# Mask rows as twelve codes, a maximum pass that writes, and last outputs in single banks

## The chip, the cores and the metric

The kernel runs on one core of a Trainium2 chip. Its time is the device time of one execution in microseconds. Three runs of the kernel before took 771.14, 771.51 and 772.78 us, so the median is 771.51. The engines are TensorE (PE, with its weight loads shown apart as PEld), VectorE (DVE), ScalarE (ACT), GpSimd (POOL) and SyncE (SP), which only issues DMAs.

## The reference

Attention over 2 batches and 8 heads of 768 tokens with 64 features, in which a query sees only keys of its own hash bucket, and then two MLPs over the 1536 tokens:

```python
q_bits = (np.einsum('bhsd,dk->bhsk', q, proj) > 0)        # 6 bits; k_bits likewise
mask = q_bucket[:, :, :, None] == k_bucket[:, :, None, :] # bucket = the 6 bits as a number
scores = np.where(mask, scale * q @ k.T, -1e9)
attn = np.exp(scores - max(scores)); attn /= attn.sum() + 1e-9
x = attn @ v
h = x @ w_in;  x = (h - tanh(h)) @ w_out                  # 512 -> 2048 -> 512
h = x @ w_in2; x = (h * sigmoid(1.702 * h)) @ w_out2
```

## The kernel before, in words

Every large product is made from numbers split in two parts, a high one in TensorE's fast 32-bit format (`xh`, `wh`, `ka`, `qa`) and the rest (`xl`, `wl`), with the product of the two rests left out.

**Attention.** The 16 heads run as eight pairs. A pair has twelve steps, one for each head and each 128 queries; 96 steps in all. In iteration `s` of the loop TensorE does in this order: the score products of step `s + 2` (`scores`, L334: four of 384 columns, the first two from `qa`/`ka`, the last two from `qb`/`kb`), two of the twelve products of probabilities and values of an earlier half pair (`pv`, L388; each shows as two matmuls), and six 128x128 transposes of the probabilities of step `s` (`transposes`, L369). VectorE takes the maximum of a step's 768 scores from PSUM (L348) and makes a bias of it (`nb`, L350). ScalarE takes the exponential from PSUM, with that bias, into `pr` in SBUF, with the sum over the row (L352), and copies the transposes from PSUM to SBUF (L377). The scores lie in one of two PSUM tiles of two banks each (tag `S`), the transposes in two single banks (tag `T`); tags `g` and `v` have a bank each. Tiles of one tag take turns, and a tile is given out again when all that reads it is done.

**The mask** is part of the score product. `qa` and `ka` hold 128 rows: the 64 features twice over in different parts. `qb` and `kb` hold 64 feature rows and, in rows 64 to 127, one row for each of the 64 buckets: a one in `kb` where the key lies in that bucket, and minus 2 to the 100 in `qb` where the query does not. A key of another bucket so gets a score of about minus 2 to the 100. The rows are made once a pair. `prep_bits` multiplies keys and queries by `proj` into a PSUM tile `pb` (L262) and compares with zero on VectorE (`bits`, L271). `prep_hot`, four times a pair, multiplies the bits with a table (`sel_sb`, loaded at the start) into a PSUM tile `po` (L293), and VectorE makes 384 columns of `kb` and of `qb` from it (L305, L308). The first pair is made another way, from a small table in bf16, and the change leaves that alone.

**Preparation of the next pair** (`prep_ahead`): at step 10 of a pair the tiles of the pair after next are loaded (`r` on SP, `ka`, `qa`, `qb` on GpSimd's queue); at step 1 GpSimd splits the rest parts off (`split_q`, `split_k`, four operations of 64x768, L238 and L244) and `prep_bits` is done; `prep_hot` follows in steps 2, 4, 5 and 7; `v` is loaded in step 7. For the second pair it is step 3 and then 4 to 7. Slices of the MLP weights are loaded and converted in between. `r` has one buffer, the others two.

**The MLPs** run over 16 slices `c` of the hidden units, eight for each layer, with 3 blocks `t` of 512 tokens and 2 halves `j` of a slice. The order of all work is a list written out by hand (`ORDER`, and `STEADY` where it has no entry): `h21` is the product into the hidden block t = 2, j = 1; `t21` its activation, `g21` the gate, `hi21` and `lo21` its two parts; `o213` the output product for t = 2, j = 1 and feature block d = 3 (or token block, in the last layer), three matmuls of 512 columns (L703); `ev23` adds the output to the sum `acc` on VectorE (L711) and, in the last slice, stores it (L714). A name with `-` belongs to the slice before. An output block's four accumulators lie in two `S` tiles, two in each. Where the list has `P`, products are combined from sums of blocks, which the change does not touch.

```python
ORDER[16] = "ev10- ev11- ev12- ev13- g21- hi21- o200- o201- o202- o203- lo21- o210- o211- "
            "o212- o213- ev20- ev21- ev22- ev23- "          # what follows the last slice
```

Of the kernel before, what the change touches and what calls it, by code (L numbers as in the profile page):

```python
# [10 lines left out]
F32 = mybir.dt.float32  # L11
F32R = mybir.dt.float32r
# [24 lines left out]
CH = 2  # L37
NCHUNK = 2 * NFC // CH
BIG = float(2.0**100)
NTAB = 98  # L40
# [17 lines left out]
def lsh_attention_then_two_mlps(  # L58
# [4 lines left out]
    rr: bass.AP,  # L63
    vv: bass.AP,
    tab: bass.AP,
    sel: bass.AP,
    eye: bass.AP,
    w1: bass.AP,
    w2: bass.AP,
# [118 lines left out]
    sel0 = tab_sb[:, 32:96].bitcast(BF16)  # L188
    pop_sb = tab_sb[:, 96:97]
    hot_sb = tab_sb[:, 97:98]  # L190
    eye_sb = cst.tile([128, 128], F32, name="eye_sb")
    sel_sb = cst.tile([128, 4, 128], F32R, name="sel_sb")

# [18 lines left out]
    def load_first():  # L212
        b, p = pairs[0]
        pair_tiles(0)
        qa, qb, ka, kb, r = heads[0]
        c0, c1 = slice(0, HALF), slice(HALF, S)
        for h in range(2):
            nc.sync.dma_start(out=r[:, h], in_=rr[b, p, :, h])
            nc.gpsimd.dma_start(out=ka[:, h], in_=kd[b, p, :, h])
            nc.gpsimd.dma_start(out=qa[:, h, c0], in_=qd[b, p, :, h, c0])  # L220
            nc.gpsimd.dma_start(out=qb[0:64, h, c0], in_=qd[b, p, 0:64, h, c0])
        nc.sync.dma_start(out=eye_sb, in_=eye)
        nc.gpsimd.dma_start(out=qa[:, :, c1], in_=qd[b, p, :, :, c1])
        nc.gpsimd.dma_start(out=qb[0:64, :, c1], in_=qd[b, p, 0:64, :, c1])
        nc.gpsimd.dma_start(out=sel_sb, in_=sel)

    def load_v(i):
        b, p = pairs[i]
# [23 lines left out]
    def prep_bits(i, hs=(0, 1), tag="g"):  # L252
        r = heads[i][4]
        pb = ps.tile([128, 512], F32, tag=tag, name=f"pb{i}_{hs[0]}")
        if hs[0] == 0:
            bits[i] = sm.tile(
                [128, HALF], F32R if i else BF16, tag=f"bits{min(i, 1)}", name=f"bits{i}", bufs=1
            )
# [11 lines left out]
        rows = slice(hs[0] * 64, hs[-1] * 64 + 64)  # L270
        nc.vector.tensor_scalar(bits[i][rows], pb[rows, :HALF], 0.0, None, op0=ALU.is_gt)  # L271

    def prep_hot(i, h, f, tag="g"):
        qa, qb, ka, kb, r = heads[i]
        c = slice(f * HALF, (f + 1) * HALF)  # L280
        g = 64 * h + 32 * f
        po = ps.tile([128, 512], F32, tag=tag, name=f"po{i}_{h}_{f}")
        if i == 0:
            nc.tensor.matmul(
                po[:, :HALF],
                sel0[g : g + 32],
                bits[i][g : g + 32],
                start=True,
                stop=True,
                tile_position=(g, 0),  # L290
            )
        else:
            nc.tensor.matmul(po[:, :HALF], sel_sb[:, g // 32], bits[i], start=True, stop=True)  # L293

        def masks():
            if i == 0:
                nc.scalar.activation(
                    kb[64:128, h, c], po[64:128, :HALF], AF.Relu, bias=hot_sb[64:128], scale=BIG
                )
                nc.vector.tensor_scalar(  # L300
                    qb[64:128, h, c], po[0:64, :HALF], pop_sb[0:64], -1.0,
                    op0=ALU.subtract, op1=ALU.max,
                )
                return
# [22 lines left out]
    def scores(s):  # L327
        u, i, f, j, h = where(s)
        qa, qb, ka, kb, _ = heads[i]
        t0 = f * UT + j * QT  # L330
        sc = ps.tile([128, 2, 512], F32, tag="S", name=f"sc{s}", bufs=2)
        for n in range(2):
            for hf in range(2):
                nc.tensor.matmul(  # L334
                    sc[:, hf, :HALF],
                    (qa, qb)[n][:, h, t0 : t0 + QT],
                    (ka, kb)[n][:, h, hf * HALF : (hf + 1) * HALF],
                    start=(n == 0),
                    stop=(n == 1),
                )  # L340
        return sc

    def softmax(s, sc):
        u, i, f, j, h = where(s)
        if s % (2 * NQ) == 0:
            sums[u] = sm.tile([128, NQ, 2], F32, tag="rs", name=f"rs{u}")
        nm = sm.tile([128, 1], F32, tag="nm", name=f"nm{s}")
        nc.vector.tensor_reduce(nm, sc[:, :, :HALF], AX.XY, ALU.max, negate=True)  # L348
        nb = sm.tile([128, 1], F32, tag="nb", name=f"nb{s}")
        nc.vector.tensor_scalar_mul(nb, nm, D**-0.5)  # L350
        pr = prp.tile([128, S], F32, tag="pr", name=f"pr{s}")
        nc.scalar.activation(  # L352
            pr.rearrange("p (a b) -> p a b", a=2), sc[:, :, :HALF], AF.Exp,
            bias=nb, scale=D**-0.5, accum_out=sums[u][:, j, h : h + 1],
        )
        prob[s] = pr

# [100 lines left out]
    PO = ((2, 4, 5, 7), (4, 5, 6, 7))  # L458
# [5 lines left out]
    masks = [prep_hot(0, 0, 0, "g"), prep_hot(0, 0, 1, "v")]  # L464
    masks[0]()
    split_q(0, 0, nc.vector, c0)
    masks[1]()
# [6 lines left out]
    for s in range(NSTEP + 2 * NQ + 1):  # L474
# [22 lines left out]
        if s < NSTEP:  # L497
            if s == 0:
                for f in range(2):
                    prep_hot(0, 1, f, "gv"[f])()  # L500
# [12 lines left out]
            convert(s, 1)  # L513
# [167 lines left out]

    def out_mm(c, t, j, d):
        first = j == (1 if t == 1 and c % LAYER else 0)
        if first and d == 0:
            oacc[c, t] = [
                ps.tile([128, 2, 512], F32, tag="S", name=f"o{c}_{t}_{i}", bufs=2)
                for i in range(2)
            ]
        hi, lo = gh[c, t, j], gl[c, t, j]
        woh, wol = wh[c, j], wl[c, j]  # L690
        o = oacc[c, t][d // 2][:, d % 2, :]
# [12 lines left out]

    def evac(c, t, d):
        o = oacc[c, t][d // 2][:, d % 2, :]
        m = acc_of(d, t)
        if c % LAYER == 0:
            nc.scalar.activation(m, o, AF.Copy)  # L709
# [48 lines left out]
    def issue(name, c):  # L758
# [39 lines left out]
        elif kind == "tab":  # L798
# [60 lines left out]
        ),  # L859
        NCHUNK: (  # L860
            "ev10- ev11- ev12- ev13- g21- hi21- o200- o201- o202- o203- lo21- o210- o211- "
            "o212- o213- ev20- ev21- ev22- ev23- "
        ),
    }
    for c in range(NCHUNK + 1):
        for name in ORDER.get(c, STEADY).split():
# [69 lines left out]
```

## Time and profile before

| | |
|---|---|
| runs (3), median | 771.51 us (771.14 to 772.78) |
| profiled execution, own time | 772.15 us |
| its span | 770.0 us |
| PE busy / DVE / ACT / POOL | 749.5 / 585.1 / 424.3 / 400.6 us |
| first score product / first MLP product | 9.45 / 257.17 us |
| last matmul starts | 764.33 us |
| reduction L348, exponential L352, mask L305 + L308 | 91.6, 87.0, 17.5 + 17.1 us |

A row of the timeline has the start, the duration, the engine, the line, the operation, the tile written and the tiles read, their shape, and in brackets how long the engine had been idle before and what ended that. Matmuls overlap, and their ends are modelled; what a matmul costs is read from the distance of starts. A row that says x2 merges two instructions that follow each other.

### The profile page before, as it was taken

The page shows a single profiled execution, that of the slowest core. Times are in us where ns is not written, and L with a number is a line of the kernel's source. Part 1 is how long each engine was busy: PE and PEld are TensorE (multiplying, and loading weights), DVE is VectorE, ACT ScalarE, POOL GpSimd, SP SyncE. Part 2 cuts the span into 40 slices and gives each one's busy share as a digit, 9 for nine tenths or more (in the row PEclk, how much of TensorE's full clock was granted, in tenths as well). Part 3 has the DMA queues.
Part 4 walks back from the last instruction along what each step waited for, and adds up shares of the span by engine and source line. Part 5 has one row for each costly group of instructions (what it writes and reads, how often), then busy time and mean ns, then how long its engine had stood idle before and what let it go on. Part 6 is the DMA issues. An engine that isn't in the chain of part 4 may idle for free.

```text
span 770.0 us, 10036 instructions
## 1 busy us (share of the span) xinstructions
PE 749.5 (97%) x3708; PEld 570.0 (74%) x3708; DVE 585.1 (76%) x840; ACT 424.3 (55%) x793; POOL 400.6 (52%) x342
## 2 busy tenths in 40 slices
PE   5899999999999999999999999999999999999996
PEld 3566666666666688888888888887888888888885
DVE  4778778767667768878887787897798778877653
ACT  3777777777778466354353543656545355353430
POOL 6451651643410586564644745699774474564620
PEclk9999999999999999999999999999999999999999
DMA  9535234043120211131112111302022211130004
GB/s 266 177 104 192 88 104 163 22 145 125 40 76 1 110 55 66 45 110 54 55 66 83 72 55 54 110 6 104 24 87 78 81 60 55 55 110 0 1 11 154
DMA packets 12993, 62.89 MB, mean 82 GB/s; under 512 B 1616, under 2 KB 2512, under 8 KB 8848
## 3 DMA queue, kind: packets, MB, share of 16 engines
q1 hardware_dynamic: 8928, 46.21, 16.7%
q0 software_dynamic: 3872, 15.99, 7.1%
q8 instruction: 29, 0.48, 0.3%
q14 instruction: 20, 0.16, 0.1%
q10 hardware_dynamic: 144, 0.05, 0.0%
HBM read 59.10 MB, written 3.15 MB: 81 GB/s over the span
## 4 chain that ended last, share of the span: by engine, by line
PE 88%; DVE 3%; POOL 2%; issue 2%; DMA 2%; ACT 1%; POOLq 0%; DVEq 0%; ACTq 0%
PE o L703 31%; PE h L614 12%; PE y L614 10%; PE pv L388 10%; PE tp L369 9%; PE sc L334 8%; PE w L614 5%; PE x L614 2%; DMA r<-in_rr 1%; DMA ka<-in_kd 1%; POOL xl L726 1%; PE rb L413 1%; PE pb L262 1%; PE po L293 1%; DVE acc L594 1%
## 5 line engine op out<-in xcount | busy, mean ns | idle before, releaser
L676 POOL TENSOR_TENSOR gl<-f,gh 128x512 fp32r<-128x512 f32 x62 | 86.2, 1390 | 162.1 <-ACT gh L671 156.7
L711 DVE TENSOR_TENSOR acc<-o,acc 128x512 f32<-128x512 f32 x168 | 108.6, 684 | 48.6 <-PE o L703 48.1
L377 ACT ACTIVATE pt<-tp 128x384 f32<-128x384 f32 x184 | 80.3, 489 | 47.9 <-PE tp L369 47.0
L348 DVE TENSOR_REDUCE nm<-sc 128x1 f32<-128x768 f32 x96 | 91.6, 954 | 14.6 <-PE sc L334 13.4
L369 PEld LDWEIGHTS tp<-eye_sb,pr 128*128 128x128 f32 x576 | 61.6, 140 | 53.5 <-issue 25.7
L145 POOL TENSOR_TENSOR wl<-w,wh 128x512 fp32r<-128x512 f32 (+1 forms) x62 | 86.4, 1405 | 19.0 <-ACT wh L142 18.9
L352 ACT ACTIVATE pr<-sc,nb 128x768 f32<-128x768 f32 x96 | 87.0, 906 | 16.0 <-DVE nb L350 8.9
L369 PE MATMUL tp<-eye_sb,pr 128*128 128x128 f32 x576 | 83.5, 281 | 0.0
L388 PE MATMUL pv<-pt,v 128*64 128x384 f32 x384 | 82.0, 510 | 0.0
L735 ACT ACTIVATE u<-y 128x512 f32<-128x512 f32 x42 | 25.2, 600 | 100.6 <-PE y L614 100.6
L703 PE MATMUL o<-wh,gh 128*128 128x512 f32 x192 | 75.0, 391 | 0.9 <-ACT acc L709 0.7
L703 PE MATMUL o<-wh,gl 128*128 128x512 f32 x192 | 74.8, 390 | 0.5 <-POOL gl L676 0.5
L703 PE MATMUL o<-gh,wh 128*128 128x512 f32 x192 | 74.8, 390 | 0.0
L703 PE MATMUL o<-wl,gh 128*128 128x512 f32 x192 | 74.7, 389 | 0.0
L703 PE MATMUL o<-gl,wh 128*128 128x512 f32 x192 | 74.7, 389 | 0.0
L703 PE MATMUL o<-gh,wl 128*128 128x512 f32 x192 | 74.7, 389 | 0.0
L614 PE MATMUL h<-xl,wh 128*128 128x512 f32 x160 | 62.4, 390 | 0.6 <-POOL xl L726 0.6
L614 PE MATMUL h<-xh,wh 128*128 128x512 f32 x160 | 62.4, 390 | 0.0
L614 PE MATMUL h<-xh,wl 128*128 128x512 f32 x160 | 62.3, 389 | 0.0
L334 PE MATMUL sc<-ka,qa 128*128 128x384 f32 x192 | 55.7, 371 | 2.3 <-DVE qa L238 1.9
L671 ACT ACTIVATE gh<-f 128x512 fp32r<-128x512 f32 x62 | 39.0, 629 | 28.7 <-DVE f L667 28.5
L334 PE MATMUL sc<-kb,qb 128*128 128x384 f32 x192 | 50.2, 342 | 2.0 <-DVE qb L300 2.0
(138 smaller groups left out, 1652.7 us busy)
## 6 DMA issues: line engine op xcount, KB each, us to landing
raw<-in_w SPq DMA_DIRECT2D x32, 1024.0 KB, 4.8
ka<-in_kd POOLq DMA_DIRECT2D x7, 768.0 KB, 4.7
qa<-in_qd POOLq DMA_DIRECT2D x7, 768.0 KB, 6.7
r<-in_rr SPq DMA_DIRECT2D x7, 768.0 KB, 4.5
v<-in_vv SPq DMA_DIRECT2D x8, 384.0 KB, 3.1
out<-acc SPq DMA_DIRECT2D x12, 256.0 KB, 2.1
qb<-in_qd POOLq DMA_DIRECT2D x7, 384.0 KB, 8.0
r<-in_rr SPq DMA_DIRECT2D x2, 384.0 KB, 4.2
```

The source lines that it names most:

```text
L145: nc.gpsimd.tensor_tensor(wl[c, j][:, f], ws[c, j][:, f], wh[c, j][:, f].bitcast(F32), ALU.subtract)
L334: nc.tensor.matmul(sc[:, hf, :HALF], (qa, qb)[n][:, h, t0 : t0 + QT], (ka, kb)[n][:, h, hf * HALF : (hf + 1) * HALF], start=(n == 0), stop ...
L348: nc.vector.tensor_reduce(nm, sc[:, :, :HALF], AX.XY, ALU.max, negate=True)
L352: nc.scalar.activation(pr.rearrange("p (a b) -> p a b", a=2), sc[:, :, :HALF], AF.Exp, bias=nb, scale=D**-0.5, accum_out=sums[u][:, j, h : ...
L369: nc.tensor.transpose(tp[:, k * 128 : (k + 1) * 128], pr[:, c * 128 : (c + 1) * 128], eye_sb)
L377: nc.scalar.activation(dst, src, AF.Copy)
L388: nc.tensor.matmul(acc[u][h * 64 : (h + 1) * 64, :UT], v[:, h, c, :], probT[u][:, c, h, :], start=(c == 0), stop=(c == NCH - 1),)
L614: nc.tensor.matmul(o, a, b, start=(start and n == 0 and m == 0), stop=(n == len(pairs) - 1 and m == 2), skip_group_check=not start,)
L671: nc.scalar.activation(gh[c, t, j], fs[c, t, j], AF.Copy)
L676: eng.tensor_tensor(gl[c, t, j], fs.pop((c, t, j)), gh[c, t, j].bitcast(F32), ALU.subtract)
L703: nc.tensor.matmul(o, a, m, start=(first and n == 0), stop=(not first and n == 2))
L711: nc.vector.tensor_tensor(m, o, m, ALU.add)
```

## The change

The 64 bucket rows of pairs 1 to 7 become twelve code rows (`NCODE`), so the second half of the score product has 76 rows instead of 128. For a key the rows are bit minus 1 (six rows) and bit (six rows), for a query bit and bit minus 1, one side times 2 to the 100: their product is minus 2 to the 100 for each bit that differs. The bits come from VectorE with the 1 already taken off (`off_sb`), GpSimd multiplies by a column of factors (`amp_sb`), and eight DMAs on SP copy twelve rows each into `kb` and `qb` (`prep_codes`). `prep_hot` remains for the first pair alone; the table `sel_sb` and its load go. `prep_bits` and `prep_codes` now stand ahead of the splits. Since several bits can differ, the scores are clamped at minus 2 to the 100: VectorE's pass writes the clamped scores into `pr` in SBUF and delivers the maximum with it, and the exponential runs in place in `pr`. In the last slice the last output block's four accumulators are single banks, and the hand-written order of that slice is another.

```diff
     def prep_bits(i, hs=(0, 1), tag="g"):
...
+        else:
+            nc.vector.tensor_scalar(
+                bits[i], pb[:, :HALF], 0.0, off_sb, op0=ALU.is_gt, op1=ALU.subtract
+            )
+    def prep_codes(i):
+        qa, qb, ka, kb, r = heads[i]
+        codes = sm.tile([128, HALF], F32, tag="codes", name=f"codes{i}", bufs=1)
+        nc.gpsimd.tensor_scalar_mul(codes, bits[i], amp_sb)
+        for h in range(2):
+            for f in range(2):
+                g = 64 * h + 32 * f
+                c = slice(f * HALF, (f + 1) * HALF)
+                for o, x in enumerate((kb, qb)):
+                    nc.sync.dma_start(
+                        out=x[64 : 64 + NCODE, h, c].bitcast(F32),
+                        in_=codes[g + o * NCODE : g + (o + 1) * NCODE],
+                    )
-            nc.vector.tensor_scalar(
-                kb[64:128, h, c], po[64:128, :HALF], pop_sb[64:128], None, op0=ALU.is_equal
-            )
-            nc.vector.tensor_scalar(
-                qb[64:128, h, c], po[0:64, :HALF], pop_sb[0:64], -BIG,
-                op0=ALU.is_lt, op1=ALU.mult,
-            )
...
     def scores(s):
+        nb = 64 + NCODE if i else 128
-                    (qa, qb)[n][:, h, t0 : t0 + QT],
-                    (ka, kb)[n][:, h, hf * HALF : (hf + 1) * HALF],
+                    (qa, qb)[n][: (128, nb)[n], h, t0 : t0 + QT],
+                    (ka, kb)[n][: (128, nb)[n], h, hf * HALF : (hf + 1) * HALF],
...
     def softmax(s, sc):
-        nm = sm.tile([128, 1], F32, tag="nm", name=f"nm{s}")
-        nc.vector.tensor_reduce(nm, sc[:, :, :HALF], AX.XY, ALU.max, negate=True)
+        pr = prp.tile([128, S], F32, tag="pr", name=f"pr{s}")
+        mx = sm.tile([128, 1], F32, tag="mx", name=f"mx{s}")
+        nc.vector.tensor_scalar(
+            pr.rearrange("p (a b) -> p a b", a=2), sc[:, :, :HALF], -BIG, None,
+            op0=ALU.max, op1=ALU.max, accum_out=mx,
+        )
         nb = sm.tile([128, 1], F32, tag="nb", name=f"nb{s}")
-        nc.vector.tensor_scalar_mul(nb, nm, D**-0.5)
-        pr = prp.tile([128, S], F32, tag="pr", name=f"pr{s}")
+        nc.vector.tensor_scalar_mul(nb, mx, -(D**-0.5))
         nc.scalar.activation(
-            pr.rearrange("p (a b) -> p a b", a=2), sc[:, :, :HALF], AF.Exp,
-            bias=nb, scale=D**-0.5, accum_out=sums[u][:, j, h : h + 1],
+            pr, pr, AF.Exp, bias=nb, scale=D**-0.5, accum_out=sums[u][:, j, h : h + 1]
         )
...
         elif k == 1 + first:
+            prep_bits(i)
+            prep_codes(i)
             for h in range(2):
                 split_q(i, h, nc.gpsimd)
                 split_k(i, h, nc.gpsimd)
-            prep_bits(i)
-        elif k in PO[i == 1]:
-            n = PO[i == 1].index(k)
-            prep_hot(i, n // 2, n % 2)()
...
     def out_mm(c, t, j, d):
-        if first and d == 0:
+        if first and d == 0 and (c, t) == (NCHUNK - 1, NTB - 1):
+            oacc[c, t] = [bank(tag, f"o{c}_{t}_{i}") for i, tag in enumerate("TTgv")]
...
+        NCHUNK - 1: (
...
+            "lo11 hi20 o000 o001 wadd t10 o002 o003 lo01 h21 g10 hi10 lo20 t21 o010 lo10 g21 "
+            "hi21 o011 lo21 o012 ev00 o013 ev01 ev02 o110 o100 ev03 o111 o101 o112 o102 ev10 "
+            "o113 o103 ev11 o200 o210 ev12 ev13 o201 o211 ev20 ev21 o202 o212 ev22 o203 o213 "
+            "ev23 "
+        ),
+        NCHUNK: "",
```

## Rows read from the trace of the kernel before

**Rows 1.** The page: busy time and share of the span; shares of the chain.

```profile
PE 749.5 (97%) x3708; PEld 570.0 (74%) x3708; DVE 585.1 (76%) x840; ACT 424.3 (55%) x793; POOL 400.6 (52%) x342
...
PE 88%; DVE 3%; POOL 2%; issue 2%; DMA 2%; ACT 1%; POOLq 0%; DVEq 0%; ACTq 0%
```

**Rows 2.** Timeline of TensorE, steady attention: start, duration, engine, line, operation.

```profile
152.12 0.59 PE L334 MATMUL sc<-ka,qa 128*128 128x384 f32 x2
...
154.42 0.42 PE L293 MATMUL po<-bits,sel_sb 128*128 128x384 f32 x1
154.68 0.51 PE L334 MATMUL sc<-ka,qa 128*128 128x384 f32 x2
...
156.90 0.59 PE L334 MATMUL sc<-ka,qa 128*128 128x384 f32 x2
...
161.85 0.59 PE L334 MATMUL sc<-ka,qa 128*128 128x384 f32 x2
...
164.15 0.59 PE L334 MATMUL sc<-ka,qa 128*128 128x384 f32 x2
```

**Rows 3.** Timelines of TensorE, VectorE and GpSimd in the first pair.

```profile
31.50 0.41 PE L293 MATMUL po<-bits,sel_sb 128*128 128x384 f32 x1 [0.77 <-DVE qb L308]
...
36.51 0.59 PE L334 MATMUL sc<-ka,qa 128*128 128x384 f32 x2
...
25.53 0.56 DVE L271 TENSOR_SCALAR bits<-pb 128x384 fp32r<-128x384 f32 x1 [2.36 <-PE pb L262]
...
28.86 0.96 DVE L348 TENSOR_REDUCE nm<-sc 128x1 f32<-128x768 f32 x1
...
31.39 0.96 DVE L348 TENSOR_REDUCE nm<-sc 128x1 f32<-128x768 f32 x1
...
24.70 1.82 POOL L238 TENSOR_TENSOR qa<-r,qa 64x768 fp32r<-64x768 f32 x1 [7.72 <-DMA r<-in_rr]
```

**Rows 4.** Timelines of TensorE and VectorE at the end of the kernel.

```profile
762.15 0.50 PE L703 MATMUL o<-wh,gl 128*128 128x512 f32 x1 [0.48 <-POOL gl L676]
...
764.33 0.39 PE L703 MATMUL o<-wh,gl 128*128 128x512 f32 x1
...
763.38 2.66 DVE L711 TENSOR_TENSOR acc<-o,acc 128x512 f32<-128x512 f32 x4 [3.30 <-PE o L703]
```

**Rows 5.** Groups by line, first 300 us: busy us, mean ns; idle before.

```profile
L348 DVE TENSOR_REDUCE nm<-sc 128x1 f32<-128x768 f32 x96 | 91.6, 954 | 14.6 <-PE sc L334 13.4 <-issue 0.3
L352 ACT ACTIVATE pr<-sc,nb 128x768 f32<-128x768 f32 x96 | 87.0, 906 | 16.0 <-DVE nb L350 8.9 <-PE sc L334 6.3 <-DVE rc L403 0.4
...
L377 ACT ACTIVATE pt<-tp 128x384 f32<-128x384 f32 x184 | 80.3, 489 | 47.9 <-PE tp L369 47.0
...
L352 ACT ACTIVATION_READ_ACCUMULATOR pr<-sc,nb 128x1 f32 x96 | 19.9, 208 | 0.0
...
L305 DVE TENSOR_SCALAR kb<-po,tab_sb 64x384 fp32r<-64x384 f32 x28 | 17.5, 624 | 10.0 <-PE po L293 9.6
L308 DVE TENSOR_SCALAR qb<-po,tab_sb 64x384 fp32r<-64x384 f32 x28 | 17.1, 610 | 0.5
L350 DVE TENSOR_SCALAR nb<-nm 128x1 f32<-128x1 f32 x96 | 14.8, 154 | 6.3
...
L421 DVE COPY rbs<-rb 128x384 f32<-128x384 f32 x16 | 8.9, 558 | 8.0 <-PE rb L413 7.6
```

**Rows 6.** The line of the stores: issue in ns, issue to landing in us.

```profile
L714 SPq DMA_DIRECT2D out<-acc x12: 332/332/577, 749.4 to 766.1; - x12
...
DMA to landing us min/median/max: 2.0/2.1/3.0
```

**Rows 7.** Groups by line of ScalarE: a copy from SBUF, one from PSUM.

```profile
L671 ACT ACTIVATE gh<-f 128x512 fp32r<-128x512 f32 x62 | 39.0, 629 | 28.7 <-DVE f L667 28.5
...
L735 ACT ACTIVATE u<-y 128x512 f32<-128x512 f32 x42 | 25.2, 600 | 100.6 <-PE y L614 100.6
```

**Rows 8.** Timeline near the end of attention: a score product that waits.

```profile
245.82 0.62 PE L334 MATMUL sc<-ka,qa 128*128 128x384 f32 x2 [0.17 <-ACT pr L352]
```

More of the change, by code (lines that the diff above doesn't have):

```diff
@@ L39 @@
 BIG = float(2.0**100)
-NTAB = 98
+NTAB = 100
+NCODE = 2 * NBITS
 F64_INF = float(np.uint32((1023 + 128) << 20).view(np.float32))
@@ L190, in lsh_attention_then_two_mlps @@
     hot_sb = tab_sb[:, 97:98]
+    off_sb = tab_sb[:, 98:99]
+    amp_sb = tab_sb[:, 99:100]
     eye_sb = cst.tile([128, 128], F32, name="eye_sb")
-    sel_sb = cst.tile([128, 4, 128], F32R, name="sel_sb")
     def pair_tiles(i):
@@ L224, in load_first @@
         nc.gpsimd.dma_start(out=qb[0:64, :, c1], in_=qd[b, p, 0:64, :, c1])
-        nc.gpsimd.dma_start(out=sel_sb, in_=sel)
     def load_v(i):
@@ L256, in prep_bits @@
             bits[i] = sm.tile(
-                [128, HALF], F32R if i else BF16, tag=f"bits{min(i, 1)}", name=f"bits{i}", bufs=1
+                [128, HALF], F32 if i else BF16, tag=f"bits{min(i, 1)}", name=f"bits{i}", bufs=1
             )
@@ L269, in prep_bits @@
                 )
-        rows = slice(hs[0] * 64, hs[-1] * 64 + 64)
-        nc.vector.tensor_scalar(bits[i][rows], pb[rows, :HALF], 0.0, None, op0=ALU.is_gt)
-    def prep_hot(i, h, f, tag="g"):
-        qa, qb, ka, kb, r = heads[i]
+        if i == 0:
+            rows = slice(hs[0] * 64, hs[-1] * 64 + 64)
+            nc.vector.tensor_scalar(bits[i][rows], pb[rows, :HALF], 0.0, None, op0=ALU.is_gt)
+        else:
+            nc.vector.tensor_scalar(
+                bits[i], pb[:, :HALF], 0.0, off_sb, op0=ALU.is_gt, op1=ALU.subtract
+            )
@@ L280, in prep_hot @@
+    def prep_hot(h, f, tag="g"):
+        qa, qb, ka, kb, r = heads[0]
         c = slice(f * HALF, (f + 1) * HALF)
         g = 64 * h + 32 * f
[L282 to L290, printed above, removed]
-            )
-        else:
-            nc.tensor.matmul(po[:, :HALF], sel_sb[:, g // 32], bits[i], start=True, stop=True)
@@ L295, in masks @@
-        def masks():
-            if i == 0:
-                nc.scalar.activation(
-                    kb[64:128, h, c], po[64:128, :HALF], AF.Relu, bias=hot_sb[64:128], scale=BIG
-                )
-                nc.vector.tensor_scalar(
[L301 to L304, printed above, removed]
-            nc.vector.tensor_scalar(
-                kb[64:128, h, c], po[64:128, :HALF], pop_sb[64:128], None, op0=ALU.is_equal
+        po = ps.tile([128, 512], F32, tag=tag, name=f"po{h}_{f}")
@@ L307, in masks @@
+        nc.tensor.matmul(
+            po[:, :HALF],
+            sel0[g : g + 32],
+            bits[0][g : g + 32],
+            start=True,
+            stop=True,
+            tile_position=(g, 0),
+        )
+        def masks():
+            nc.scalar.activation(
+                kb[64:128, h, c], po[64:128, :HALF], AF.Relu, bias=hot_sb[64:128], scale=BIG
             )
             nc.vector.tensor_scalar(
-                qb[64:128, h, c], po[0:64, :HALF], pop_sb[0:64], -BIG,
-                op0=ALU.is_lt, op1=ALU.mult,
+                qb[64:128, h, c], po[0:64, :HALF], pop_sb[0:64], -1.0,
+                op0=ALU.subtract, op1=ALU.max,
@@ L463, in lsh_attention_then_two_mlps @@
     split_k(0, 0, nc.vector)
-    masks = [prep_hot(0, 0, 0, "g"), prep_hot(0, 0, 1, "v")]
+    masks = [prep_hot(0, 0, "g"), prep_hot(0, 1, "v")]
     masks[0]()
@@ L499, in lsh_attention_then_two_mlps @@
                 for f in range(2):
-                    prep_hot(0, 1, f, "gv"[f])()
+                    prep_hot(1, f, "gv"[f])()
             elif s == 1:
@@ L683, in out_mm @@
         first = j == (1 if t == 1 and c % LAYER else 0)
-        if first and d == 0:
+        if first and d == 0 and (c, t) == (NCHUNK - 1, NTB - 1):
+            oacc[c, t] = [bank(tag, f"o{c}_{t}_{i}") for i, tag in enumerate("TTgv")]
+        elif first and d == 0:
             oacc[c, t] = [
-                ps.tile([128, 2, 512], F32, tag="S", name=f"o{c}_{t}_{i}", bufs=2)
+                o[:, i]
+                for o in (
+                    ps.tile([128, 2, 512], F32, tag="S", name=f"o{c}_{t}_{n}", bufs=2)
+                    for n in range(2)
+                )
                 for i in range(2)
@@ L690, in out_mm @@
         woh, wol = wh[c, j], wl[c, j]
-        o = oacc[c, t][d // 2][:, d % 2, :]
+        o = oacc[c, t][d]
         if c < LAYER:
@@ L705, in evac @@
     def evac(c, t, d):
-        o = oacc[c, t][d // 2][:, d % 2, :]
+        o = oacc[c, t][d]
         m = acc_of(d, t)
@@ L890 @@
     pp = np.zeros((128, 32), proj.dtype)
-    pp[0:64, 0:NBITS] = proj
-    pp[64:128, NBITS : 2 * NBITS] = proj
+    off = np.zeros((128, 1), np.float32)
+    amp = np.ones((128, 1), np.float32)
+    for n in range(2):
+        pp[0:64, n * NBITS : (n + 1) * NBITS] = proj
+        pp[64:128, NCODE + n * NBITS : NCODE + (n + 1) * NBITS] = proj
     sel = np.zeros((128, 128), np.float32)
     pop = np.zeros((128, 1), np.float32)
+    for g in range(0, 128, 32):
+        off[g : g + NBITS] = 1
+        off[g + NCODE + NBITS : g + 2 * NCODE] = 1
+        amp[g : g + NCODE] = BIG
     for bk in range(NBUCKET):
@@ L907 @@
     tab[:, 97:98] = BIG * (1.0 - pop)
-    sel4 = np.zeros((128, 4, 128), np.float32)
-    for g in range(4):
-        sel4[32 * g : 32 * g + 32, g] = sel[32 * g : 32 * g + 32]
+    tab[:, 98:99] = off
+    tab[:, 99:100] = amp
     arrays = {
```

9 lines of the change are left out of this document (2 added, 7 removed), and 3 rows, old and new, of the table ORDER.

## The prediction

> **What bounds the kernel now.** I read the page's busy times and its chain of waits first: the reader is to see that TensorE carries the end, with 97% of the span and 88% of the chain, while VectorE has 76%, ScalarE 55% [rows 1]. A busy TensorE in this view is not TensorE at its peak, so the second view is its timeline in the attention stage, read by starts alone. One step (four score products, four probability-times-value products, six transposes) goes from one first score product to the next in 2.30 us (161.85 to 164.15), with no wait named on any row: the steady step is TensorE's own [rows 2]. A step that carries one product into the mask tile `po` starts its successor after 2.56 us (152.12 to 154.68) and the next one comes after 2.22 (to 156.90): 4.78 against 4.60 for two plain steps, so one `po` costs TensorE 0.18 us, far less than the 0.42 that its own row states [rows 2]. The third view, timelines of the first pair, shows another bound: there the score reductions of VectorE start 2.53 us apart (28.86, 31.39), back to back with two mask operations, and TensorE waits 0.77 us for `qb` [rows 3]. The fourth is the end: a wait of 0.48 us for `gl`, and four additions of which the last ends 1.32 us behind the last matmul (763.38 + 2.66 = 766.04 against 764.33 + 0.39) [rows 4].
>
> **The change, part by part.** The sum is made against the profiled execution: 770.0 us of span, 772.15 in its own time, 0.64 above the median of 771.51.
>
> *Mask rows, steady pairs.* Seven pairs lose four `po` products, 28 in all, and 28 `kb` and 28 `qb` operations with them: 17.5 + 17.1 = 34.6 us of VectorE [rows 5]. On the path stand TensorE's 0.18 x 4 = 0.72 us a pair. Six of the seven are prepared while a steady pair runs: 6 x 0.72 = 4.3 us. Ends: 3.6 (0.15 each, if a step keeps some of the room) and 4.9 (0.20). What is late next is again TensorE: the plain step of 2.30 is what remains.
>
> *Mask rows, first pair.* Its four prepared steps run at VectorE's 2.53. Without the masks VectorE needs about 1.3 a step (below). ScalarE then needs two copies and one exponential, 2 x 489 + 906 less some 0.03 of overlap, about 1.85 [rows 5]. Two of the four steps have no value products and go at ScalarE's 1.85, two have them and go at TensorE's 2.30: 8.3 against 10.1, 1.8 us, and the step ahead of them loses its own `po` of 0.18: 2.0 us. Ends: 0.7 (only the four products) and 2.4.
>
> *What is added for them.* GpSimd scales the bits, 128x384 once a pair: between nothing and the 1.82 of one of its splits, which have two inputs and twice the columns [rows 3]; I take half of that, 0.9. It stands ahead of four splits, so these now wait for the bits. In the first prepared pair they start at 24.70 now, when `r` lands [rows 3]; then at 27.0 (the bits end at 26.1, then the scaling), and the last, four times 1.85 later, ends at 34.4. That pair's first score product comes in the step after 36.51 [rows 3], by my sum at about 37.3. So nothing waits, with 2.9 us to spare. Then SP issues eight copies of 12 rows. Its stores show 0.33 to 0.58 for an issue, eight of them 2.7 to 4.6, and 2.0 to 3.0 to landing [rows 6]: from 27.0 to 34.6 at worst. What queues behind them on SP is the next `v` (wanted six steps into the pair after) and the next `r`, which waits for the splits anyway, as now; it goes out about 2.4 us later and has ten us in hand. In steady pairs the preparation begins nine steps of 2.3 ahead, some 20 us, against a chain of 0.9 + 4.6 + 3.0. All of it hidden: 0. If that cover were gone, TensorE would wait at the head of each pair by the lateness.
>
> *76 rows for 128 in the second score product.* It streams the same 384 columns. The trace has nothing of 76 rows, and no row that gives a sign; I take 0. The nearest row is the 128-row product into `po` with its 0.18 of real pitch. A tenth of that on the 168 products (two a step, 84 steps) would be 3.0 us either way, and 0.05 each would use up the gain.
>
> *Maximum pass that writes.* The reduction (96 x 954 ns) becomes a clamp that writes 128x768 and delivers the maximum [rows 5]. Not in the trace. Below: 0.61, the mask operation, which takes half the columns. Above: reduction plus two 128x384 copies from PSUM, 954 + 2 x 558 = 2.07. I take 0.96, the reduction's own: the 558 of a copy shows that one that writes 384 columns runs at about the pace of the reduction (half of 954 is 477, plus a fixed part). ScalarE's exponential reads its accumulator out in a second instruction of 208 ns, most of it overlapped [rows 5]; I add 0 to 0.21, 0.1 taken. [...] With `nb` at 0.15 VectorE has 1.2 to 1.3 a step against 2.30: free, and the lost mask operations (8 x 0.61 a pair) more than pay for it.
>
> *Exponential in SBUF.* ScalarE's 128x512 copies take 629 from SBUF and 600 from PSUM [rows 7]; so 906 becomes at most 0.95 (29 more for 512 columns, 44 for 768), and at least 0.90 if the size has no part in it. ScalarE's step of 1.9 stays below 2.30; in the two fast steps it costs 0.1, which the sum leaves out. [...] The score banks come free behind the clamp, not behind the exponential. Only the last pair shows TensorE waiting for that, once, with 0.17 idle [rows 8], and there ScalarE runs almost without a gap: I take 0.2, from 0 to 0.5.
>
> *The end.* The new order of the last slice puts both halves of an output next to each other, with `gl` made earlier: the 0.48 of named wait, about 0.6 with the restart, goes [rows 4]. Now two 0.68 additions follow the last matmul, since two outputs share one tile; with single banks one does: 0.7. The stores of 256 KB land after 2.1 in the median and 3.0 in the longest case, and the last four go out within 2.7 us [rows 4, 6]; with 1.4 us between them (two products of three matmuls) I take 0.5 for the last one (0 to 0.9). A new wait: the second output block follows the first with no `h` between, and needs two additions (1.3) beside two products of 0.68: about 0.1, covered. Together 1.8, from 1.0 to 2.5. The mask table that is no longer loaded is last in its queue: 0.
>
> Sum: 4.3 + 2.0 + 0.2 + 1.8 = 8.3 us. From 772.15: 763.85; from the median 771.51: **763.2**.
>
> **Rivals.** *A, another wait takes the place of part of the gain* (the exponential late behind a longer VectorE chain, the tail's additions late for the next bank). For: the transposes are marked with waits on `pr` in the trace. Against: these rows are weight loads issued ahead, and the plain step holds 2.30. The low ends of the terms with half the tail: 3.6 + 0.7 + 0 + 0.9 = 5.2: 766.3.
>
> *B, VectorE becomes the bound: slower.* If the clamp costs the sum of reduction and copies, 2.07 + 0.21 + 0.15 = 2.43 a step. A pair at TensorE's pace is twelve steps, 30.0 now and 29.3 after, and VectorE's other work in it is some 3.1 (bits 0.56, two copies and two products of about that, two short reciprocals). So it decides from (29.3 - 3.1) / 12 = 2.18 us a step, twice what the reduction and `nb` take now (1.11). At 2.43: 12 x 2.43 + 3.1 = 32.3, 2.3 more than now in each of eight pairs: +18, about 790. Against: no row of VectorE costs near two passes.
>
> *C, the code rows come late.* SP is in order, and copies wait behind GpSimd, which waits for the bits. For 7 heads to lose 1.2 us each, as much as the change gains, the copies would need 20 us instead of 8; then no change, 771.5.
>
> **How the numbers follow.** The forecast has 0.70 (its own range 761.2 to 765.0, the upper ends of all terms giving 10.3 saved), A 0.19, B 0.05, C 0.04, and 0.02 for what I do not see, slower. A measurement tells some 0.2% from no change, 1.5 us. Faster 0.89, same 0.04, slower 0.07. The range reaches over A: 760.8 to 767.2.
>
> **What would show it.** Right: steady pairs of twelve steps in 29.3 instead of 30.0, plain steps still 2.30; the four steps of the first pair at about 1.9 and 2.3; a clamp near 0.96 and VectorE with some 24 us less work; last addition about 0.7 behind the last matmul, no wait for `gl`. Wrong: a clamp over 2 us, a wait of TensorE on a code copy or on `kb`/`qb` at the head of a pair, score products with another pitch than 0.18, or a transpose that waits for the exponential in every step.

## The result, and the profile after

The changed kernel takes 763.14 us (median; 762.95 to 763.83) against 772.0 for the kernel before on the same chip: ratio 0.9887, 95% interval 0.987 to 0.9904. The forecast was 763.2, which is 8.3 below a median of 771.51; with a fourth run that median is 772.0, and 8.9 were gained. That the two times agree to 0.1 is therefore partly luck. The profiled execution took 763.3, with a span of 761.3 (before: 770.0).

TensorE still carries the end, with more of the chain than the 88% before [rows 1]. From the page after, busy times and the chain's shares:

```profile
PE 743.8 (98%) x3680; PEld 565.0 (74%) x3680; DVE 553.8 (73%) x880; ACT 427.1 (56%) x793; POOL 408.6 (54%) x348
...
PE 91%; DVE 3%; POOL 1%; ACT 1%; DMA 1%; issue 1%; DVEq 0%; ACTq 0%; POOLq 0%
```

VectorE has 31 us less, TensorE 5.7, which is not yet the gain of 8.7. The groups by line, first 300 us (busy us, mean ns; idle before), answer to [rows 5]:

```profile
L352 DVE TENSOR_SCALAR_CACHE_REDUCE pr<-sc 128x768 f32<-128x768 f32 x96 | 91.7, 956 | 37.6 <-PE sc L337 35.6 <-ACT pt L382 0.2 <-issue 0.2
L358 ACT ACTIVATE pr<-pr,nb 128x768 f32<-128x768 f32 x96 | 90.0, 937 | 11.4 <-DVE nb L357 11.0
...
L358 ACT ACTIVATION_READ_ACCUMULATOR pr<-pr,nb 128x1 f32 x96 | 19.0, 198 | 0.0
L357 DVE TENSOR_SCALAR nb<-mx 128x1 f32<-128x1 f32 x96 | 14.8, 154 | 3.3
L281 POOL TENSOR_SCALAR codes<-bits,tab_sb 128x384 f32<-128x384 f32 x7 | 8.7, 1243 | 18.2 <-DVE bits L274 9.3 <-issue 9.0
L352 DVE DVE_READ_ACCUMULATOR pr<-sc 128x1 f32 x96 | 8.0, 83 | 0.0
```

The clamp that writes 768 columns costs what the reduction did (956 against 954 ns). Behind it stands a second instruction of 83 ns that the reduction did not need, but it makes nothing later: from the start of the pass to the start of the bias `nb` it is 1.00 us in the median of the 96 steps, in both kernels. VectorE's idle time ahead of the pass, waiting for scores, went from 14.6 to 37.6 us: outside the first pair VectorE lost work and nobody noticed but VectorE.

The gain is found by distances of starts on TensorE, here the first score products of the twelfth step of the first pair and of two later pairs:

```profile
34.54 0.59 PE L337 MATMUL sc<-ka,qa 128*128 128x384 f32 x2
...
63.87 0.59 PE L337 MATMUL sc<-ka,qa 128*128 128x384 f32 x2
...
93.21 0.59 PE L337 MATMUL sc<-ka,qa 128*128 128x384 f32 x2
```

The first stood at 36.51 before [rows 3]. From 63.87 to 93.21 a pair takes 29.34; in the kernel before, by the same two steps, 30.01:

```profile
66.88 0.59 PE L334 MATMUL sc<-ka,qa 128*128 128x384 f32 x2
...
96.89 0.59 PE L334 MATMUL sc<-ka,qa 128*128 128x384 f32 x2
```

The end, with one addition behind the last matmul and no wait for `gl` [compare rows 4], on TensorE and on VectorE:

```profile
757.23 0.39 PE L711 MATMUL o<-wh,gl 128*128 128x512 f32 x1
```

```profile
756.30 0.69 DVE L719 TENSOR_TENSOR acc<-o,acc 128x512 f32<-128x512 f32 x1 [0.67 <-PE o L711]
757.66 0.69 DVE L719 TENSOR_TENSOR acc<-o,acc 128x512 f32<-128x512 f32 x1 [0.67 <-PE o L711]
```

Where the 8.7 us of span came from, by distances that leave out when the first score product starts (9.45 and 9.48) and the MLPs up to the last slice's outputs (0.05 apart):

| stretch | before | after | gain | forecast |
|---|---|---|---|---|
| first pair, to its twelfth score product | 27.05 | 25.06 | 1.99 | 2.0 |
| six pairs behind that, each 30.01 and 29.34 | 180.0 | 176.0 | 4.0 | 4.3 |
| one wait at the head of the second pair (3.02 and 2.63 a step) | | | 0.38 | none |
| last pair, then end of attention to the first MLP product | 28.91 + 11.35 | 28.36 + 11.90 | 0.0 | 0.2 |
| first product of the last slice's outputs to the end of the span | 25.62 | 23.25 | 2.37 | 1.8 |

### The profile page after: what moved, and what is told of

It is laid out like the page before. It is cut to its first block, busy times and chain, and to the rows that moved or that the text cites. A ratio compares the mean times of both kernels' runs of the same rounds, so it can differ in the third digit from the quotient of the medians.

```text
span 761.3 us, 10133 instructions
## 1 busy us (share of the span) xinstructions
PE 743.8 (98%) x3680; PEld 565.0 (74%) x3680; DVE 553.8 (73%) x880; ACT 427.1 (56%) x793; POOL 408.6 (54%) x348
## 4 chain that ended last, share of the span: by engine, by line
PE 91%; DVE 3%; POOL 1%; ACT 1%; DMA 1%; issue 1%; DVEq 0%; ACTq 0%; POOLq 0%
PE o L711 33%; PE h L616 12%; PE y L616 10%; PE pv L393 10%; PE tp L374 9%; PE sc L337 8%; PE w L616 5%; PE x L616 3%; DMA r<-in_rr 1%; POOL xl L734 1%; PE pb L262 1%; PE rb L418 1%; DVE acc L596 1%; DVE w L121 0%; DVE acc L719 0%
## 5 line engine op out<-in xcount | busy, mean ns | idle before, releaser
L352 DVE TENSOR_SCALAR_CACHE_REDUCE pr<-sc 128x768 f32<-128x768 f32 x96 | 91.7, 956 | 37.6 <-PE sc L337 35.6
L358 ACT ACTIVATE pr<-pr,nb 128x768 f32<-128x768 f32 x96 | 90.0, 937 | 11.4 <-DVE nb L357 11.0
L337 PE MATMUL sc<-ka,qa 128*128 128x384 f32 x192 | 57.9, 383 | 2.1 <-DVE qa L238 2.1
L337 PE MATMUL sc<-kb,qb 76*128 76x384 f32 (+1 forms) x192 | 50.6, 344 | 2.1 <-DVE qb L310 2.1
```

The costliest lines, as they stand in the source:

```text
L337: nc.tensor.matmul(sc[:, hf, :HALF], (qa, qb)[n][: (128, nb)[n], h, t0 : t0 + QT], (ka, kb)[n][: (128, nb)[n], h, hf * HALF : (hf + 1) * H ...
L352: nc.vector.tensor_scalar(pr.rearrange("p (a b) -> p a b", a=2), sc[:, :, :HALF], -BIG, None, op0=ALU.max, op1=ALU.max, accum_out=mx,)
L358: nc.scalar.activation(pr, pr, AF.Exp, bias=nb, scale=D**-0.5, accum_out=sums[u][:, j, h : h + 1])
```

## The experiments

Each ran beside the kernel before. Ratios and their intervals are to that one; differences in us are between medians of runs from different times. The median of the kernel before lies between 771.58 and 772.03 in them, so a few tenths between two medians settle nothing by themselves.

**The end.** Both put back, and then the order alone.

```diff
-        if first and d == 0 and (c, t) == (NCHUNK - 1, NTB - 1):
-            oacc[c, t] = [bank(tag, f"o{c}_{t}_{i}") for i, tag in enumerate("TTgv")]
...
-        NCHUNK - 1: (
...
-        NCHUNK: "",
+        NCHUNK: (
+            "ev10- ev11- ev12- ev13- g21- hi21- o200- o201- o202- o203- lo21- o210- o211- "
...
```

> The changed kernel with its end put back: the last slice in the old order, its last output block in two tiles of two banks. By my sum the end is worth 1.8 us (0.6 for the wait for gl, 0.7 for one addition, 0.5 for the stores); by the two traces, from the first output product of the last slice to the end of the span, 25.62 against 23.2, it is 2.4. So this should come out at about 765.5 us (764.9 to 765.8) and leave 6.0 to 6.5 of the gain to attention. Rival: the end gains nothing by itself, the shorter attention merely moves it and the stores: then it stays at 763.1.

764.86 us, ratio 0.9912 (0.9899 to 0.9926): the end is worth 1.7, just under what was expected, and the rest, 7.2 against the 772.02 of the kernel before in the same runs, belongs to attention. With the new order but two-bank tiles (only the part of the edit on `oacc`):

> The changed kernel with the new order of the last slice, but its last output block in two tiles of two banks as before. My sum gives the order the wait for gl (0.6), and the single banks the addition (0.7) and the shorter landing (0.5): then this comes out at 764.3 us (763.1 + 1.2). If the order alone does it, 763.1 to 763.4, and the fourth accumulator's bank is worth nothing; if the banks do all of it, 765.5, as with the old end.

764.21, ratio 0.9903 (0.9888 to 0.9918): 0.65 for the order and 1.07 for the banks, near the forecast of 0.6 and 1.2. The executions overlap (764.41 to 766.42 with the old end, 763.79 to 764.90 with the order alone, 762.95 to 763.83 with both), so the medians alone do not show the split. The traces do: from the first output product to the start of the last addition it is 21.02 with the old end, 20.63 with the order alone and 19.56 in the changed kernel, so 0.39 and 1.07. The reason is another than the forecast one. TensorE near the end, in the version with the order alone:

```profile
755.26 0.39 PE L709 MATMUL o<-wh,gl 128*128 128x512 f32 x1
756.43 0.50 PE L709 MATMUL o<-wh,gh 128*128 128x512 f32 x1 [0.78 <-DVE acc L717]
...
757.69 0.40 PE L709 MATMUL o<-wh,gl 128*128 128x512 f32 x1
```

There too a single addition follows the last matmul (758.12 + 0.69): that comes with the order. What the banks take away is a wait of TensorE: the last accumulator shares its tile with one that VectorE is still adding, and its first matmul comes 1.17 after the one before it, where 0.23 is the pitch. From the first to the last matmul of the last slice's outputs it takes 20.20, the changed kernel 19.13 and the kernel before 19.93: the order alone trades the wait for `gl` for a longer one, and the banks take that one, 1.07.

In the trace the old end costs 24.80 from the first output product to the end of the span, not the 25.62 of before. The stretch up to the last addition's start is the same (21.02 and 20.97); from the end of that addition to the end of the span it is 3.10 instead of 3.97, and 3.00 in the changed kernel. So of the 2.37 in the table 1.4 belong to matmuls and additions (20.97 against 19.56); the rest is the landing, which with the old end is 3.10 here and 3.97 in the profile of before, so that two profiles don't size it.

**The clamp: not there, and alone.**

```diff
...
-        nc.vector.tensor_scalar(
-            pr.rearrange("p (a b) -> p a b", a=2), sc[:, :, :HALF], -BIG, None,
-            op0=ALU.max, op1=ALU.max, accum_out=mx,
-        )
+        nc.vector.tensor_reduce(nm, sc[:, :, :HALF], AX.XY, ALU.max, negate=True)
...
```

> The changed kernel with the maximum pass and the exponential as before: a reduction that writes nothing, the exponential from PSUM. Left out is the clamp, so a query whose bucket holds no key is not treated as in the reference. My theory costs the clamp nothing beside TensorE: 763.1, within 0.5; it may gain 0.03 x 4 in the first pair, where ScalarE sets the step, and lose 0.2 at the end of attention. Rival (part of the gain eaten by the longer VectorE and ScalarE chain): 760.5 to 762, faster by what the clamp eats.

763.10, ratio 0.9886 (0.9872 to 0.9899). The other way round, the old kernel with that edit reversed:

> The kernel before with one part of the change: the maximum pass writes the clamped scores and the exponential runs in place. The mask, with 128 rows and its four products a pair, and the end stay as before. My theory: 771.5 to 772.5 us, no change against 772.0: 0.08 of accumulator read x 4 in the first pair, which VectorE sets there at 2.53 a step, is the only place where it is on the path. Rival (VectorE has no room beside its mask operations): in the mask steps VectorE has 0.96 + 0.08 + 0.15 + 1.23 = 2.4 against TensorE's 2.48, so a few tenths for 24 steps, 774 to 778.

771.55, ratio 0.9994 (0.9985 to 1.0003). In both, the medians show nothing gained and nothing lost, and the rival that a longer chain eats part of the gain falls. Inside it is not nothing. Without the clamp TensorE, in the first pair, waits for the exponential that still reads the scores:

```profile
27.43 0.62 PE L337 MATMUL sc<-ka,qa 128*128 128x384 f32 x2 [0.31 <-ACT pr L355]
```

The four steps from 25.51 to 33.75 then take 8.24 (1.92, 1.73, 2.29, 2.30); the changed kernel takes 7.72 for them, with no such wait. So here the clamp gains 0.5, and the six steady pairs are together 0.3 shorter with it. In this execution `r` came early: the product of the bits, which needs it, starts 14.36 behind the first score product instead of 15.18, and that covers the difference. Why the medians do not show it stays open; executions of either version differ by 0.5 to 0.9. At the end of attention two things cancel. With the clamp alone the last pair's score products no longer wait for the exponential [rows 8] (last two steps 2.30 and 2.30, before 2.38 and 2.73), and the last pair takes 28.29 instead of 28.91. But from its last score product to the first MLP product it is then 11.89 instead of 11.35: what follows does not hang on the score products. Without the clamp it is the old pair of numbers again, 28.94 and 11.35.

**VectorE loaded.** The change's pass split in two, a reduction and a clamp.

```diff
...
+        nc.vector.tensor_reduce(nm, sc[:, :, :HALF], AX.XY, ALU.max, negate=True)
         nc.vector.tensor_scalar(
-            pr.rearrange("p (a b) -> p a b", a=2), sc[:, :, :HALF], -BIG, None,
-            op0=ALU.max, op1=ALU.max, accum_out=mx,
+            pr.rearrange("p (a b) -> p a b", a=2), sc[:, :, :HALF], -BIG, None, op0=ALU.max
         )
...
```

> The changed kernel with the maximum and the clamp as two VectorE passes over the scores (a reduction, then a clamp that writes). It tests the point from which I said that VectorE decides, 2.18 us a step. A reduction 0.95 and a clamp without maximum of some 0.9 to 0.96, with 0.15 for the bias, are 2.0 to 2.1 a step, 12 x 2.05 + 3.1 = 27.7 of the 29.3 us of a pair: by my break-even it stays at 763 to 765 in steady pairs and loses only in the first pair, 4 x 0.3 = 1.2: 764 to 766. If waiting for VectorE begins earlier than the sum of its busy times says (each step's chain is reduction, bias, exponential, transposes in turn, and the score banks are held longer), it loses 0.2 to 0.7 a step over 84: 780 to 820.

769.22, ratio 0.9965 (0.9953 to 0.9978): 6.1 lost of 8.9 gained, between the two ranges expected. A step is 2.04 us of VectorE by busy times (0.95 + 0.95 + 0.14), and starts are 1.79 apart where it does nothing else (107.39 and 109.18): both under the 2.18 from which VectorE was to decide. Pairs in which VectorE converts no MLP weights keep to the sum: 29.40 and 29.47. The others take 29.7 to 30.3, and there the sum had left out 3.4 to 3.8 us a pair of VectorE's weight conversions and of transposes that it copies. Even with it VectorE is busy 27.7 of 30.33:

```profile
66.50:96.83 30.33, 29.64 (x185) 18.30 (x184) 27.67 (x49) 22.95 (x52) 15.52 (x13) 1.00 0.43 144
```

(columns: stretch, length, busy us and count of PE, PEld, DVE, ACT, POOL, then granted clock and DMA). VectorE, ScalarE and TensorE in the middle of that pair:

```profile
73.19 1.22 DVE L136 SCALAR_TENSOR_TENSOR w<-raw,w 128x1024 f32<-128x1024 f32 x1
74.32 0.95 DVE L352 TENSOR_REDUCE nm<-sc 128x1 f32<-128x768 f32 x1
75.19 0.95 DVE L353 TENSOR_SCALAR pr<-sc 128x768 f32<-128x768 f32 x1
```

```profile
76.29 0.94 ACT L358 ACTIVATE pr<-pr,nb 128x768 f32<-128x768 f32 x1 [1.60 <-DVE nb L357]
77.13 0.18 ACT L358 ACTIVATION_READ_ACCUMULATOR pr<-pr,nb 128x1 f32 x1
77.22 1.04 ACT L142 ACTIVATE wh<-w 128x1024 fp32r<-128x1024 f32 x1
78.17 0.84 ACT L382 ACTIVATE pt<-tp 128x384 f32<-128x384 f32 x2
```

```profile
78.69 0.93 PE L374 MATMUL tp<-eye_sb,pr 128*128 128x128 f32 x6 [0.69 <-ACT pt L382]
```

VectorE has no gap from 65.43 to 80.23; the conversion of 1.22 in it makes the maximum late, ScalarE stands 1.60 for it, then does its own weight copy first, and TensorE waits for the transposes' tile. So VectorE decides before its mean is full. The first pair lost 2.15 (27.21 against 25.06), of which only 0.62 lie behind the product of the bits; ahead of it TensorE's wait for VectorE's `qb` is 3.0 instead of 2.08, but this execution's mean granted clock is also the lowest of the five, 0.996 (0.999 in the changed kernel's profile), so that share need not be VectorE's alone.

**The cover of the code rows.** Scaling and copies at step 8 instead of 1; bits and splits as they are.

```diff
         elif k == 1 + first:
             prep_bits(i)
-            prep_codes(i)
...
+        if k == 8:
+            prep_codes(i)
```

> The changed kernel with the code rows made at step 8 of a pair instead of step 1 (step 3), the bits and the splits as they are. It takes away the cover on which I cost the code rows at nothing. The first score product of the next pair is two steps on, 4.6 us. The chain to it is the scaling of 1.24, four issues of 0.76 each (the first head's copies) and 2 to land: 6.3, behind what else GpSimd does in step 8 (about 1). So 2 to 3 us late at the head of each of seven pairs: 777 to 784 us, with TensorE waiting there for a copy into kb or qb. Rival: nothing is late, as GpSimd and SP run ahead of TensorE: 763.1.

765.20, ratio 0.9911 (0.9898 to 0.9925): 2.1 lost, not 14 to 21, and for another reason. At the head of the second pair TensorE does wait for a copy, 0.46, and at no other pair's: at the third pair GpSimd scales from 61.48, SP issues the third copy at 64.46, and the product that needs it starts at about 67.4. GpSimd came to it 0.9 ahead of TensorE's step, where I had put it 1 behind, and three copies are wanted first, not four. The larger loss is at an innocent transfer. SP's queue and then TensorE, around the fifth pair:

```profile
127.16 0.71 SPq L287 DMA_DIRECT2D qb<-codes  x1
127.91 0.51 SPq L207 DMA_DIRECT2D r<-in_rr  x1
```

```profile
136.92 0.85 PE L262 MATMUL pb<-r,tab_sb 128*32 128x384 f32 x8 [1.15 <-DMA r<-in_rr]
```

The next `r` stands behind eight copies on SP; in the changed kernel it went out at 117.86. It arrives late, and `prep_bits` holds all of TensorE for it. The step that carries `prep_bits` takes 4.80 there and 3.45 and 3.37 in two other pairs, against 3.25.

**76 rows.** The second score product over 128 rows again, the rest of them zeros.

```diff
...
+        for x in (kb, qb):
+            nc.gpsimd.dma_start(out=x[64 + NCODE :], in_=zz)
...
-        nb = 64 + NCODE if i else 128
+        nb = 128
...
```

> The changed kernel with the second half of the score product over 128 rows again: the 52 rows behind the twelve codes are zeros, loaded once per pair and tile by two DMAs on GpSimd's queue. I cost 76 rows against 128 at nothing: 763.1 within 0.5. If the fewer rows are why the fourth score product's successor comes 184 ns after it instead of 175 (0.01 a step, 0.05 a pair), this is 0.3 faster in steady pairs; if fewer rows make a product cheaper, it is slower by up to 3 us.

768.25, ratio 0.9948 (0.9934 to 0.9961), 5.1 slower; but that is its added load. TensorE in its first pair, and the distance of two steps twelve apart:

```profile
28.39 1.51 PE L265 MATMUL pb<-r,tab_sb 128*32 128x384 f32 x8 [6.16 <-DMA r<-in_rr]
...
69.40 0.59 PE L340 MATMUL sc<-ka,qa 128*128 128x384 f32 x2
...
98.69 0.59 PE L340 MATMUL sc<-ka,qa 128*128 128x384 f32 x2
```

Two zero blocks of 312 KB, issued at 14.81 and 15.36 and landing 9.4 and 11.4 later, are under way beside `r`, which is issued at 17.91, and the wait for it goes from 2.44 to 6.16; the first pair takes 30.46 instead of 25.06. Of these 5.4 the later `r` makes 3.6; the other 1.8 are lost behind it, where TensorE's products, after its stand of 6.16, go at the pace that other runs show at a granted clock of 0.50 (1.01 and 0.97 for two score products at 29.83 and 32.41, for 0.62 and 0.59 in the changed kernel). The steady pair takes 29.287 and the last 28.293, where 76 rows take 29.340 and 28.360. Fewer rows do not make the product cheaper; in these traces they cost 0.05 a pair, 0.4 in all.

**Towards a faster version.** Two waits of TensorE stand out in the changed kernel's first pair, as in the kernel before: one of 2.08 for `qb`, and this one, which was 1.97 before:

```profile
24.66 0.85 PE L262 MATMUL pb<-r,tab_sb 128*32 128x384 f32 x8 [2.44 <-DMA r<-in_rr]
```

```diff
-        first = 2 if i == 1 else 0
+        first = 4 if i == 1 else 0
```

> The changed kernel with the second pair prepared at step 5 instead of step 3. In its trace, as in the one before, TensorE stands 2.44 us in the first pair, before the product of the bits, until r has landed; two steps later r is there. If that wait is on the path, this gains 2 to 2.4 us: 760.7 to 761.2. Against it: the code rows and splits now come two steps (4 us) later, the last split at about 39 instead of 35, and the second pair's first score product is at 37.2: part of the gain may come back there as a wait of 1 to 3 us (762 to 764).

763.32 (762.25 to 763.61), ratio 0.9886 (0.9871 to 0.9901): no gain, though the wait is gone and no new one came. And the weights:

```diff
-    AT1 = (2, 4, 6, 8, 8, 10)
+    AT1 = (2, 3, 4, 5, 6, 7)
```

> The changed kernel with the weight slices of the first MLP slice loaded and converted earlier in the last pair (steps 2 to 7 instead of 2 to 10). In the changed kernel's trace the last conversion on VectorE (1.75 us) stands ahead of the clamp of one of the last steps, and from there the chain runs through exponential and transposes; the end of attention gave back 0.55 us of the last pair's gain. If that conversion is the cause: 0.5 to 0.9 faster, 762.2 to 762.6. If it is ScalarE's own chain of exponentials and copies: no change, 763.1.

762.63 (762.46 to 764.66), ratio 0.9886 (0.9872 to 0.9899). In the trace the end of attention is 0.30 shorter (11.60 against 11.90), less than expected; the runs cannot tell that from none. Both edits:

> Both of these edits together, as a version that may beat both kernels: 760.2 us if both waits are on the path, 762 to 764 if the second pair's late rows eat the first.

762.44 (760.87 to 765.26), ratio 0.9881 (0.9864 to 0.9898). Its profiled execution, at 760.87, shows what hid the gain of the first edit. Windows of TensorE in the version with the second pair later, and then with both edits (columns as above, granted clock third from the end):

```profile
18.00:21.00 3.00, 2.12 (x9) 2.03 (x10) 2.18 (x5) 1.08 (x3) 0.00 (x0) 0.61 1.17 311
21.00:24.00 3.00, 3.00 (x20) 2.93 (x20) 1.46 (x5) 2.78 (x7) 0.00 (x0) 0.82 0.99 378
```

```profile
18.00:21.00 3.00, 2.92 (x21) 2.86 (x22) 2.58 (x7) 1.89 (x5) 0.00 (x0) 1.00 1.16 277
21.00:24.00 3.00, 2.92 (x20) 2.13 (x19) 2.13 (x7) 3.00 (x8) 0.00 (x0) 1.00 0.99 399
```

TensorE's rows in the same order, two of each version:

```profile
13.67 1.01 PE L337 MATMUL sc<-ka,qa 128*128 128x384 f32 x2
...
18.88 1.01 PE L337 MATMUL sc<-kb,qb 128*128 128x384 f32 x2 [2.05 <-DVE qb L310]
```

```profile
13.54 0.63 PE L337 MATMUL sc<-ka,qa 128*128 128x384 f32 x2
...
18.07 0.62 PE L337 MATMUL sc<-kb,qb 128*128 128x384 f32 x2 [2.08 <-DVE qb L310]
```

The code of this stretch is the same in both. In one execution TensorE's granted clock fell to 0.50 (1.00 from 17 to 18 us, 0.84 from 18 to 19, 0.50 from 19 to 22) while TensorE stood 2.05 us for `qb`; in the other it stood 2.08 and the clock stayed at 1.00. From the first of these rows to the first score product of the third step behind it took 9.08 in one and 6.92 in the other. Not all of that follows the fall: 0.70 are lost in the step at 13.67 already, whose products have the pace of those at 0.50 (1.01 for two, though the clock reads 1.00 there), and 1.46 in the two steps around the fall. Behind them 0.3 comes back, so the twelfth score product is 24.99 behind the first instead of 23.16. Both versions again, on one chip (the 2.54 that is named below is the step at 13.67):

> The changed kernel once more, beside the version with both edits on the same chip. TensorE's granted clock falls to 0.50 for some 4 us at about 18 us in some executions and not in others, and the wait for r that follows takes that up (in the profiles with the old end and with the new order alone the wait is shorter by as much). So this should scatter little: 763.1, all executions within 0.5.

> The version with both edits once more. Without the wait for r nothing takes up a low clock at 18 us, which costs 1.8 us there (three steps of 2.54, 1.94 and 1.94 against 1.84, 1.46 and 1.35): executions at full clock at 760.9 to 761.3, the others at 762.5 to 763.2, so a median between them, 0 to 2 us below the changed kernel's. Rival: the second wait was not on the path, and both versions have the same median, 763.1.

The changed kernel: 762.86 (762.67 to 762.99), ratio 0.9887 (0.987 to 0.9903), whether its mean granted clock was 0.997 or 1.0. Both edits: 760.58, 760.93 and 761.11 at 0.999 to 1.0, and 763.06 at 0.997; median 761.02, ratio 0.9869 (0.9854 to 0.9884). In the changed kernel's profile of these runs the clock falls too (0.69 from 18 to 21 us, 0.74 from 21 to 24), and the wait for `r` behind it is 1.17 instead of 2.44: the wait takes the low clock up. So the version with both edits is the fastest here by median, 1.8 us ahead of the changed kernel on that chip, but the two intervals overlap. With the runs above, its nine executions reach from 760.58 to 765.26 with a median of 762.0, the eight of the changed kernel from 762.67 to 763.83 with 763.0: a lead is likely, its size is not settled. That an execution's share of it depends on the clock fits the four runs; among the five above, one took 762.44 at a mean clock of 1.0 and one 765.26 at 0.997, so the clock is not all of it. Why the clock falls in one and not in the other stays open.

## Why the prediction was right, step by step

- **TensorE bounds the steady pairs, and a `po` costs it 0.18**: right. 0.667 a pair came out, for 0.72; the missing 0.053 is what the 76-row products cost, which the prediction put at nothing for want of a row that gives a sign: with 128 rows a pair takes 29.287, 0.72 less than before. The code rows were not run without the clamp that they need; their gain is what the runs on the end and the clamp leave over.
- **First pair at ScalarE's pace**: 1.99 for 2.0, but two errors of the sum cancel. The prediction put the four prepared steps at four times VectorE's 2.53, 10.1, before, and at 8.3 after; they took 9.48 between score products and take 7.72 (1.36, 1.76, 2.31, 2.30; forecast 1.85, 1.85, 2.30, 2.30), 0.6 less each time. The step ahead of them took 1.64 and takes 1.38. Before, VectorE's four did take 10.06 (its reductions start at 26.39 and 36.45), but part of its lateness reached TensorE only behind them: the 0.38 at the head of the second pair, which was not foreseen. There the product of `rb` names a wait of 0.17 for ScalarE's `wide`, which is made from VectorE's reciprocal of 37.59; that this is all of the 0.38 was not tested. After, ScalarE's exponentials start 1.67 apart (27.79 and 29.46), not 1.85, and the score banks come free behind the clamp, so TensorE's first step does not wait for the exponential. Without the clamp it does, and the four steps take 8.24.
- **Clamp, accumulator read, exponential**: 956 + 83 for 0.96 + 0.1, of which the 83 delay nothing; VectorE's busy time falls by 31 us and not by 24, as these reads overlap the passes (one starts at 20.83, where its pass runs from 19.94 to 20.90); the exponential is 31 ns longer (937 against 906), for 29 in ScalarE's copies of 512 columns [rows 7]. The accumulator reads are 96 instructions of VectorE's own in the trace after. In the medians they cost nothing, as the two experiments on the clamp show.
- **0.2 at the end of attention**: the mechanism was there (score banks free behind the clamp, 0.6 in the last pair), the gain was not: what ends the stage is the chain behind the scores. That only the last pair shows such a wait was a misreading: the first pair before has one of 0.31 at 21.02, ahead of the wait for `r`.
- **Code rows hidden**: right in the outcome, wrong in the numbers. The scaling is 1.24 and not 0.9, an issue 0.71 and not 0.33 to 0.58, so the eight of the first pair end at 34.2. The moved edit showed that the cover is deep for the rows themselves, and that what the issues endanger is `r` behind them, which the prediction had seen as "ten us in hand".
- **The end, 1.8**: right in size, 1.7 between medians. Of its parts the gain of the banks was given to the last addition and the stores; the runs show a wait of TensorE in its place, and the single last addition comes with the order. So the total agrees by luck in part.
- **Rivals**: A fell with the two clamp experiments. B's price was right in kind, but its point of 2.18 was too high: it left out VectorE's weight conversions and copies of transposes, 3.4 to 3.8 us a pair, and waiting began at 2.04 busy a step wherever weights are converted beside it. C costs 2.1 with the rows seven steps later (five in the first pair), and most of that through `r`.

## What to carry to other kernels

What a step costs the bounding engine is the distance of its neighbours' starts with and without it, not its row's duration (here 0.18 for a `po` whose row says 0.42). Before adding work to an engine that looks free, add up its work in the fullest pair, not in a plain one, and look at what is queued behind each new instruction, DMA issues included. A wait that can be removed may have been covering something else: check that the gain arrives in the median and not only in one trace.

## What the runs showed of the hardware

- SP's issue of a copy of 12 rows from SBUF to SBUF, 18 KB, takes 714 ns in the median of 56 and up to 1103; that of a store of 128 rows, 256 KB, 332 [rows 6].
- A VectorE pass over 128x768 in PSUM costs the same whether it only reduces (954), only clamps and writes (948), or does both (956); the accumulator read of 83 behind the last does not delay what follows (1.00 us from start to start with and without it).
- A score product over 76 rows is not faster than one over 128; twelve steps are 0.05 us longer with it (29.340 against 29.287).
- After stands of TensorE of much the same length (2.05 and 2.08 us) the granted clock was 0.50 in one execution (second pair later, from 19 to 22 us) and 1.00 in another (both edits), with the same code up to there.
